# A shared PSUM bank, reordered maxima and query transposes, and other weight loads in a fused attention, expert and gated-product kernel

## The chip, the cores and the metric

One core of one Trainium2 chip runs the whole program. The metric is the device time of one execution, in microseconds. A profiled execution gives a trace: each instruction of TensorE (PE), VectorE (DVE), ScalarE (ACT) and GpSimd (POOL) with its start and duration, and the DMAs that SyncE (SP) issues.

## What is computed

Three parts follow one another; the output of each is the input of the next.

```python
# attention: q, k, v are 2 x 8 x 576 x 64 (batch, heads, positions, 64)
q_d, k_d, v_d = means of q, k, v over 4 neighbouring positions    # 144 positions
out_d = softmax(q_d @ k_d.T / 8) @ v_d, repeated 4 times
out_local = softmax(q @ k.T / 8 where |i - j| < 4, else -1e9) @ v
x = (out_up + out_local) as 1152 tokens x 512
# experts: 8 of them, w1 512 x 1024, w2 1024 x 512
P = exp(x @ w_gate - max);  8 times: P /= row sums; P /= column sums; P *= 1152 / 8
x = sum over e of P[:, e] * (relu(x @ w1[e]) @ w2[e])
# gated product, inner width 1536
out = (x @ w_a) * (x @ w_b) @ w_out
```

## The kernel before

**Precision.** All is float32 outside. For the large products each operand is split into a high part (rounded to fp32r) and a low part (what is left); a product is three matmuls. A piece of weights, `raw`, becomes its two parts in `split` (L134): ScalarE copies the high part (L138), VectorE or GpSimd subtracts it (L139).

**Attention as 24 orders.** An order is one batch, one third of the 576 positions and a pair of heads. The generator `side` (L1268) works them off as a software pipeline of steps s = 0, 1, 2 ...; a step is two halves, and in it several orders are at different stages:

- `a1(s)`: TensorE transposes queries (`qn`, L991) and, when a head pair is new, keys (`kn`, L1005); `a2` (ScalarE) copies them to `qT`, `kT`; `a3` (VectorE) sums four neighbours (`kd`, L1049; `qT`, L1034); `a4` (ScalarE) scales the keys' sums (`kd`, L1060).
- `b1`, `b1c`: TensorE's mask, band scores and coarse scores (all at L61, the one line of `mm`). `b2(s-1)`: VectorE's negated maxima `nm` (L1090) and `nd` (L1093). `b3(s-1)`: ScalarE's exponentials `p` (L1100) and `pd` (L1103).
- `b4(s-2)`: VectorE's sums `rsum` (L1112, L1113) and reciprocals `rr` (L1116); GpSimd multiplies `p` by them (L1117), VectorE `pd`, which gives `pdn` (L1120).
- `c1(s-2)`: TensorE transposes `pdn` (L1130) and `p` (L1135), into two PSUM banks; `c2` and `c3` copy them to `pdT` (L1141) and `plT` (L1149).
- `d1(s-3)`: eight products of `pdT` (into columns 192 to 239 of one bank) and twelve of `plT` (into its columns 0 to 191). `d2a`: ScalarE's `od` (L1170) is a quarter of the columns from 192; `d2`: VectorE's `x` (L1176) adds it to columns 0 to 191. `d3` splits `x` into `xh` (ScalarE, L1186) and `xl` (GpSimd).

So within step s TensorE does `d1(s-3)` and right after it `c1(s-2)`, and ScalarE does `d2a(s-3)` and then `b3(s-1)`. Up to TURN = 11 the scores stand in the first half of a step (`b1(s-1)`), from there on in the second, `b1(s)` in front of `d1` and `b1c(s)` behind it.

**Banks.** The attention's tiles in PSUM have the tag `at`, of 6 banks that go round; 2 more belong to the experts' first products (`g`). A tile of 512 float32 is one bank. An instruction that writes into a bank taken anew waits for the last readers of what lay there.

**What fills TensorE.** The first two half experts ("units" 0 and 1) begin while the attention runs: once tokens are ready, `step` (L1492) works through experts' tiles, calls half a step of `side` from time to time and, by the list `share` (L1490), so many tasks from the queue of weight splits (`run_first`). Loads of weights are asked for one piece per half step in `load_some` (L230), from lists that `halves` and `queue_plain` (L245) make; a piece is half the rows of a 512 x 512 block, two loads of 128 x 512 elements (or 128 x 2 x 256 for the very first unit).

Engines take their instructions strictly in the order of the program; a tile's readers and writers on other engines are kept apart by semaphores.

Of the kernel before, what the change touches and what calls it, by code (L numbers as in the profile page):

```python
# [20 lines left out]
def attn_moe_glu_kernel(  # L21
# [208 lines left out]
    def load_some():  # L230

        if nsteps[0] >= max(6, freed[0] + 2):
            fetch()
        while coming and not coming[0].dmas:
            coming.pop(0)
        if coming and nsteps[0] not in NO_LOAD:
            coming[0].dmas.pop(0)()
# [7 lines left out]
    def queue_plain(u, uses=6, low=None):  # L245

        u.w = {}
        rs = halves(u.load1, (2, 2))
        for i in range(2):
            for j in range(2):  # L250
                def piece(i=i, j=j):
                    b = u.w[i, j] = new_block(uses)
                    split(b, rs[j].tile[:, :, 256 * i:256 * i + 256], 2, low)
                    rs[j].used()
                wq.append(Task(piece, 0.0 if low else 0.68, 1.35 if low else 0.0, ready=rs[j].ready, slot=True))
# [161 lines left out]

    units = []
    for e in range(E):
        for hf in range(2):  # L420
            u = Unit()
            u.e, u.hf = e, hf
            load = loader if units else half_loader
            u.load1 = load(w1[e][:, hf * 512:(hf + 1) * 512].rearrange("(k p) f -> p k f", p=128))
            u.load2 = loader(w2[e][hf * 512:(hf + 1) * 512, :].rearrange("(k p) f -> p k f", p=128))
            units.append(u)
# [557 lines left out]
    pA, pB, pC, pD = {}, {}, {}, {}  # L984

    def a1(i, b, u, hp):
# [3 lines left out]
        for j in range(2):  # L990
            nc.tensor.transpose(  # L991
                pq[:, j * 96:(j + 1) * 96], qn[:, j].rearrange("p h d -> p (h d)"), ident[:96, :96]
            )
        pk = pk2 = None
# [113 lines left out]
    def b4(i, b, u, hp):  # L1108
        p, pd, rs = pB[i]
        rr = at.tile([128, NC + 1], F32, tag="rr", name="rr", bufs=2)  # L1110
        out_ = at.tile([R, SD], F32, tag="pdn", name="pdn", bufs=2)
# [7 lines left out]
        )  # L1119
        nc.vector.tensor_scalar_mul(  # L1120
# [4 lines left out]
    def c1(i, b, u, hp):  # L1125
        p, pd = pB.pop(i)
        pt = psa.tile([128, 512], F32, tag="at", name="at")
        pt2 = psa.tile([128, 512], F32, tag="at", name="at")
# [23 lines left out]
    def d1(i, b, u, hp):  # L1152
        a, d = pC.pop(i)
        hs = slice(2 * hp, 2 * hp + 2)
        ps = psa.tile([128, 512], F32, tag="at", name="at")
        n = NC * 16
# [111 lines left out]
    def side():  # L1268
# [17 lines left out]
        for s in range(n + 5):  # L1286
# [13 lines left out]
            do(a1, s)  # L1300
# [8 lines left out]
            if not last:  # L1309
                do(d3, s - 4)  # L1310
            do(b2, s - 1)
            do(a3, s)
# [14 lines left out]
            do(b3, s - 1)  # L1327
            do(c1, s - 2)
# [44 lines left out]
    with tc.manual_schedule():  # L1373
# [34 lines left out]
        for u, low in zip(units[:2], (nc.gpsimd, None)):  # L1408
            queue_plain(u, low=low)
# [80 lines left out]
        share = [0, 0, 1, 1, 1, 1, 2, 2, 1, 2, 1]  # L1490
# [207 lines left out]
```

## Time and profile before

| | us |
|---|---|
| runs | 1049.03, 1402.92, 1048.74; median 1049.03 |
| the profiled execution, its own time | 1048.58 |
| its span, first to last instruction | 1046.8 |
| TensorE busy | 1037.9 (99%) |
| VectorE, GpSimd, ScalarE busy | 656.1, 528.3, 481.1 |
| granted clock of TensorE, mean | 1.000 |

The profile gives for each engine the time in which it executed instructions. TensorE's matmuls overlap one another (a row of the timeline takes in several, so its end can lie behind the next row's start), so the rows' starts say more than their ends. In a timeline, "[0.91 <-ACT pd L1103]" behind a row is the time for which the engine stood idle before it and what released it. The granted clock is a share of full speed.

### The profile page before, as it was taken

The numbers are of one execution on the slowest core, as the hardware profiler recorded it, in microseconds if no ns is written. First come the engines' busy times: TensorE is split into PE (matmuls) and PEld (weight loads), VectorE is DVE, ScalarE is ACT, GpSimd is POOL, SyncE is SP. The second block draws the span as 40 slices with busy tenths as digits, with TensorE's granted clock in tenths as the row PEclk, the third lists the DMA queues.
The fourth block names the chain that finished last, engine by engine and source line by source line (L and its number), as shares of the span: only waits on it lengthen the run. The fifth ranks groups of instructions, "written<-read, shape, count | busy, mean of one in ns | idle before, by whom it ended". The sixth has DMA issues, their size and how long they took to land.

```text
span 1046.8 us, 18525 instructions
## 1 busy us (share of the span) xinstructions
PE 1037.9 (99%) x6940; PEld 937.7 (90%) x6940; DVE 656.1 (63%) x1328; ACT 481.1 (46%) x1173; POOL 528.3 (50%) x531
## 2 busy tenths in 40 slices
PE   8999999999999999999999999999999999999998
PEld 6888889899899998999899899989999899999997
DVE  7785548666566565656656565656444685767664
ACT  6764424555444444445444454544343744332320
POOL 5633136647464555647364564746444544655521
PEclk9999999999999999999999999999999999999999
DMA  9662001243323323242433323232110101221102
GB/s 194 149 165 62 10 1 41 71 132 94 117 80 115 102 71 106 66 129 83 112 104 88 106 67 113 95 113 82 61 61 21 41 21 61 61 61 41 34 8 90
DMA packets 80728, 84.53 MB, mean 81 GB/s; under 512 B 35328, under 2 KB 54784, under 8 KB 80640
## 3 DMA queue, kind: packets, MB, share of 16 engines
q1 hardware_dynamic: 78864, 82.92, 27.4%
q8 instruction: 54, 0.88, 0.3%
q10 hardware_dynamic: 1776, 0.44, 0.2%
q14 instruction: 34, 0.28, 0.1%
HBM read 71.54 MB, written 11.80 MB: 80 GB/s over the span
## 4 chain that ended last, share of the span: by engine, by line
PE 95%; DVE 2%; POOL 1%; ACT 1%; issue 1%; DMA 0%; DVEq 0%; ACTq 0%; POOLq 0%
PE g L61 90%; PE at L61 3%; PE at L1130 1%; PE at L1135 1%; PE g L855 0%; PE at L991 0%; POOL w L139 0%; PE at L1005 0%; DVE G L696 0%; ACT p L1100 0%; DMA raw<-w 0%; POOL gl L692 0%; DVE kd L1049 0%; DVE b L621 0%; DVE rsum L1112 0%
## 5 line engine op out<-in xcount | busy, mean ns | idle before, releaser
L61 PE MATMUL g<-w,gh 128*128 128x512 f32 x1314 | 408.0, 392 | 0.0
L61 PE MATMUL g<-xh,w 128*128 128x256 f32 (+2 forms) x1472 | 316.0, 300 | 0.0
L692 POOL TENSOR_TENSOR gl<-G,gh 128x256 fp32r<-128x256 f32 (+1 forms) x216 | 177.8, 832 | 250.1 <-ACT gh L690 244.0
L61 PEld LDWEIGHTS g<-w,gh 128*128 128x128 f32 x1314 | 239.6, 188 | 43.6
L61 PE MATMUL g<-w,gl 128*128 128x512 f32 x657 | 257.6, 392 | 0.0
L61 PEld LDWEIGHTS g<-xh,w 128*128 128x128 f32 x1472 | 242.8, 188 | 2.4
L61 PE MATMUL g<-xl,w 128*128 128x256 f32 (+2 forms) x736 | 220.0, 299 | 0.0
L696 DVE TENSOR_TENSOR G<-g,G 128x256 f32<-128x256 f32 (+1 forms) x400 | 168.3, 451 | 68.6 <-PE g L61 34.5
L61 PE MATMUL g<-Th,w 128*128 128x256 f32 (+1 forms) x960 | 207.5, 294 | 0.4 <-DVE G L696 0.3
L139 DVE TENSOR_TENSOR w<-raw,w 128x512 fp32r<-128x512 f32 x129 | 116.2, 910 | 79.4 <-ACT w L138 79.3
L61 PEld LDWEIGHTS g<-Th,w 128*128 128x128 f32 x960 | 159.7, 188 | 3.3 <-issue 1.0
L548 DVE SCALAR_TENSOR_TENSOR acc<-g,P,acc 128x512 f32<-128x512 f32 x126 | 94.2, 748 | 94.9 <-PE g L61 91.6
L61 PEld LDWEIGHTS g<-w,gl 128*128 128x128 f32 x657 | 123.4, 188 | 26.3
L61 PE MATMUL g<-Tl,w 128*128 128x256 f32 (+1 forms) x480 | 140.7, 293 | 0.0
L61 PEld LDWEIGHTS g<-xl,w 128*128 128x128 f32 x736 | 138.2, 188 | 2.6 <-issue 0.2
L690 ACT CAST gh<-G 128x256 fp32r<-128x256 f32 (+1 forms) x216 | 93.6, 433 | 100.7 <-DVE G L706 85.7
L138 ACT CAST w<-raw 128x512 fp32r<-128x512 f32 x181 | 109.6, 620 | 63.4 <-POOL raw L269 48.3
L688 ACT ACTIVATE G<-G 128x256 f32<-128x256 f32 (+1 forms) x168 | 74.2, 442 | 103.1 <-DVE G L696 103.1
L139 POOL TENSOR_TENSOR w<-raw,w 128x512 fp32r<-128x512 f32 x52 | 68.5, 1324 | 57.7 <-ACT w L138 57.7
L61 PEld LDWEIGHTS g<-Tl,w 128*128 128x128 f32 x480 | 90.3, 188 | 2.1
L381 POOL TENSOR_TENSOR dec<-dec 128x384 int32<-128x384 int32 x48 | 49.4, 1029 | 77.7 <-ACT dec L357 52.3
L139 POOL TENSOR_TENSOR w<-s,w 128x512 fp32r<-128x512 f32 x40 | 55.6, 1391 | 21.1 <-ACT w L138 21.0
(179 smaller groups left out, 990.9 us busy)
## 6 DMA issues: line engine op xcount, KB each, us to landing
raw<-in_moe_w_dram SPq DMA_DIRECT2D x128, 256.0 KB
w<-dec SPq DMA_DIRECT2D x48, 192.0 KB
dec<-in_moe_w_a_dram SPq DMA_DIRECT2D x16, 384.0 KB
dec<-in_moe_w_b_dram SPq DMA_DIRECT2D x16, 384.0 KB
dec<-in_moe_w_out_dram SPq DMA_DIRECT2D x16, 384.0 KB
raw<-w SPq DMA_DIRECT2D x48, 128.0 KB
raw<-w SPq DMA_DIRECT2D x12, 256.0 KB
out_dram<-acc SPq DMA_DIRECT2D x9, 256.0 KB
```

What stands on the lines that cost most here:

```text
L61: nc.tensor.matmul(out=o, lhsT=l, rhs=r, start=start, stop=stop, skip_group_check=not check)
L138: nc.scalar.copy(out=hi, in_=raw)
L139: lows.append(lambda: (low or nc.vector).tensor_tensor(out=lo, in0=raw, in1=hi.bitcast(F32), op=ALU.subtract))
L381: nc.gpsimd.tensor_tensor(out=t, in0=t, in1=raw[:, :, 0], op=ALU.add)
L548: nc.vector.scalar_tensor_tensor(out=a, in0=ps, scalar=P[:, tt, u.e:u.e + 1], in1=a, op0=ALU.mult, op1=ALU.add)
L688: nc.scalar.activation(out=src, in_=src, func=AF.Relu)
L690: nc.scalar.copy(out=h, in_=src)
L692: nc.gpsimd.tensor_tensor(out=l, in0=src, in1=h.bitcast(F32), op=ALU.subtract)
L696: nc.vector.tensor_tensor(out=o, in0=bank_, in1=b, op=ALU.add)
L1130: nc.tensor.transpose(pt2[0:72, kh * 128:kh * 128 + R], pd.rearrange("p (t k) -> p k t", k=2)[:, kh], ident[:R, :R],)
L1135: nc.tensor.transpose(pt[0:W, c * 128:(c + 1) * 128], p[:, c], ident)
```

## The change

- **One bank fewer.** `d1(i)` leaves its bank in `shared[i + 1]`, and `c1(i + 1)` writes the pdn transposes into columns 256 to 511 of it instead of into a bank of its own.
- **Maxima in front of pdn.** The multiplication that makes `pdn` is a stage of its own, `b4d`; in steps below TURN it comes behind `b2`, from there on in front of it as before.
- **Next queries in front of the probabilities.** `a1` keeps the two query transposes, `a1k` has the keys; in steps 1 to 9 `a1(s + 1)` stands in front of `c1(s - 2)`.
- **Loads.** Unit 1's first weights come by halves of the columns (`column_loader`, rows of 1 KB), so that each of the four blocks of the split needs one load piece; after half step 2 * TURN + 1 two loads are asked for at a time; `share` is another list.

```diff
--- before.py
+++ after.py
@@ -234,7 +234,9 @@
         while coming and not coming[0].dmas:
             coming.pop(0)
         if coming and nsteps[0] not in NO_LOAD:
-            coming[0].dmas.pop(0)()
+            for _ in range(2 if nsteps[0] > 2 * TURN + 1 else 1):
+                if coming[0].dmas:
+                    coming[0].dmas.pop(0)()
 
     def halves(load, left):
 
@@ -242,7 +244,7 @@
         lq.extend(rs)
         return rs
 
-    def queue_plain(u, uses=6, low=None):
+    def queue_plain(u, uses=6, low=None, columns=False):
 
         u.w = {}
         rs = halves(u.load1, (2, 2))
@@ -250,9 +252,16 @@
             for j in range(2):
                 def piece(i=i, j=j):
                     b = u.w[i, j] = new_block(uses)
-                    split(b, rs[j].tile[:, :, 256 * i:256 * i + 256], 2, low)
-                    rs[j].used()
-                wq.append(Task(piece, 0.0 if low else 0.68, 1.35 if low else 0.0, ready=rs[j].ready, slot=True))
+                    if columns:
+                        r = rs[i]
+                        raw = r.tile[:, j].rearrange("p (k f) -> p k f", k=2)
+                    else:
+                        r = rs[j]
+                        raw = r.tile[:, :, 256 * i:256 * i + 256]
+                    split(b, raw, 2, low)
+                    r.used()
+                r = rs[i if columns else j]
+                wq.append(Task(piece, 0.0 if low else 0.68, 1.35 if low else 0.0, ready=r.ready, slot=True))
 
     def queue_combined(u, low=None):
 
@@ -415,12 +424,23 @@
 
         return load
 
+    def column_loader(src):
+        def load(t, i):
+            d = t.rearrange("p a (b c) -> p (a b) c", b=2)
+            return [
+                lambda k=k: nc.sync.dma_start(
+                    out=d[:, 2 * k:2 * k + 2], in_=src[:, 2 * k:2 * k + 2, 256 * i:256 * i + 256]
+                ) for k in range(2)
+            ]
+
+        return load
+
     units = []
     for e in range(E):
         for hf in range(2):
             u = Unit()
             u.e, u.hf = e, hf
-            load = loader if units else half_loader
+            load = (half_loader, column_loader)[len(units)] if len(units) < 2 else loader
             u.load1 = load(w1[e][:, hf * 512:(hf + 1) * 512].rearrange("(k p) f -> p k f", p=128))
             u.load2 = loader(w2[e][hf * 512:(hf + 1) * 512, :].rearrange("(k p) f -> p k f", p=128))
             units.append(u)
@@ -981,7 +1001,7 @@
         )
         v_d[b, hp] = vd
 
-    pA, pB, pC, pD = {}, {}, {}, {}
+    pA, pB, pC, pD, shared = {}, {}, {}, {}, {}
 
     def a1(i, b, u, hp):
 
@@ -991,6 +1011,10 @@
             nc.tensor.transpose(
                 pq[:, j * 96:(j + 1) * 96], qn[:, j].rearrange("p h d -> p (h d)"), ident[:96, :96]
             )
+        pA[i] = pq
+
+    def a1k(i, b, u, hp):
+        pq = pA[i]
         pk = pk2 = None
         if not i:
             warm(1)
@@ -1108,7 +1132,6 @@
     def b4(i, b, u, hp):
         p, pd, rs = pB[i]
         rr = at.tile([128, NC + 1], F32, tag="rr", name="rr", bufs=2)
-        out_ = at.tile([R, SD], F32, tag="pdn", name="pdn", bufs=2)
         nc.vector.tensor_reduce(out=rs[:, 0:NC], in_=p_[i % 2], axis=AX.X, op=ALU.add)
         nc.vector.tensor_reduce(
             out=rs[0:R, NC:NC + 1], in_=pd_in[i % 2].rearrange("p g t -> p (g t)"), axis=AX.X, op=ALU.add
@@ -1117,6 +1140,11 @@
         nc.gpsimd.tensor_tensor(
             out=p, in0=p, in1=rr[:, 0:NC].unsqueeze(2).to_broadcast([128, NC, W]), op=ALU.mult
         )
+        pB[i] = p, pd, rr
+
+    def b4d(i, b, u, hp):
+        p, pd, rr = pB[i]
+        out_ = at.tile([R, SD], F32, tag="pdn", name="pdn", bufs=2)
         nc.vector.tensor_scalar_mul(
             out=out_.rearrange("p (g t) -> p g t", g=3), in0=pd, scalar1=rr[0:R, NC:NC + 1]
         )
@@ -1124,8 +1152,11 @@
 
     def c1(i, b, u, hp):
         p, pd = pB.pop(i)
+        pt2 = shared.pop(i, None)
+        if pt2 is None:
+            pt2 = psa.tile([128, 512], F32, tag="at", name="at")
+        pt2 = pt2[:, 256:512]
         pt = psa.tile([128, 512], F32, tag="at", name="at")
-        pt2 = psa.tile([128, 512], F32, tag="at", name="at")
         for kh in range(2):
             nc.tensor.transpose(
                 pt2[0:72, kh * 128:kh * 128 + R],
@@ -1153,6 +1184,8 @@
         a, d = pC.pop(i)
         hs = slice(2 * hp, 2 * hp + 2)
         ps = psa.tile([128, 512], F32, tag="at", name="at")
+        if i + 1 < len(order):
+            shared[i + 1] = ps
         n = NC * 16
         pd_ = ps[:, UT:UT + n]
         for kh in range(2):
@@ -1297,7 +1330,9 @@
             if s in LOAD_V:
                 load_v(LOAD_V[s])
             last = s >= 4 and (s - 3) % (2 * HP) == 0
-            do(a1, s)
+            if s in (0, 1) or s >= TURN:
+                do(a1, s)
+            do(a1k, s)
             if s <= TURN:
                 do(b1, s - 1)
                 do(b1c, s - 1)
@@ -1308,7 +1343,11 @@
             do(b4, s - 2)
             if not last:
                 do(d3, s - 4)
+            if s >= TURN:
+                do(b4d, s - 2)
             do(b2, s - 1)
+            if s < TURN:
+                do(b4d, s - 2)
             do(a3, s)
             if s >= TURN:
                 scale.append(lambda: do(a4, s))
@@ -1325,6 +1364,8 @@
                 do(b1c, s)
             do(d2a, s - 3)
             do(b3, s - 1)
+            if 1 <= s < TURN - 1:
+                do(a1, s + 1)
             do(c1, s - 2)
             do(d2, s - 3)
             do(c2, s - 2)
@@ -1406,7 +1447,7 @@
 
 
         for u, low in zip(units[:2], (nc.gpsimd, None)):
-            queue_plain(u, low=low)
+            queue_plain(u, low=low, columns=u is units[1])
         for u in units[:2]:
             queue_out(u)
         queue_combined(units[2], nc.gpsimd)
@@ -1487,7 +1528,7 @@
         tmp_stack = ExitStack()
         turn = 0.0
         nside = 0
-        share = [0, 0, 1, 1, 1, 1, 2, 2, 1, 2, 1]
+        share = [0, 0, 1, 1, 3, 1, 1, 1, 2, 1, 1]
 
         def step():
             nonlocal turn
```

The order on TensorE in the fourth step (s = 3), around the transposes of `pdn`, first before and then after the change (lines shift by 20 to 33; L1011 and L1161 are what L991 and L1130 were):

```order
L61 MATMUL at<-plT,vw 64x64 x2
L1130 MATMUL at<-ident,pdn 72x112 [waits DVE_49,PE_49]
L1130 MATMUL at<-ident,pdn 72x112
L1135 MATMUL at<-ident,p_115 70x128 [waits Pool_49]
L1135 MATMUL at<-ident,p_115 70x128 x2
L991 MATMUL at<-ident,qn 128x96 [waits DMAHW1_49,DMAHW0_49,PE_49]
L991 MATMUL at<-ident,qn 128x96
```

```order
L61 MATMUL at<-plT,vw 64x64 x2
L1011 MATMUL at<-ident,qn 128x96 [waits DMAHW1_49,DMAHW0_49,PE_49]
L1011 MATMUL at<-ident,qn 128x96
L1161 MATMUL at<-ident,pdn 72x112 [waits DVE_49,Activation_49]
L1161 MATMUL at<-ident,pdn 72x112
L1166 MATMUL at<-ident,p_115 70x128 [waits Pool_49]
L1166 MATMUL at<-ident,p_115 70x128 x2
```

The next step's query transposes moved ahead of the first pdn transpose, and this one waits for a semaphore of ScalarE where it waited for one of its own engine.

On VectorE, in the fifth step (s = 4), the reductions to `nm` and `nd` and the multiplication to `pdn`, before and after:

```order
L1116 RECIPROCAL rr<-rsum_120 128x4 [waits DVE_49]
L1120 TENSOR_SCALAR pdn<-pd_116,rr 112x144 [waits DVE_49]
L1090 TENSOR_REDUCE nm<-at 128x3 [waits PE_49]
L1093 TENSOR_REDUCE nd<-at 112x1
L1049 TENSOR_REDUCE kd_446<-kT_429 128x144 [waits Activation_49]
L1034 TENSOR_REDUCE qT_112<-qT_112 128x48 [waits Activation_49]
L1176 TENSOR_TENSOR x<-at,od 128x192 [waits Activation_49]
```

```order
L1139 RECIPROCAL rr<-rsum_120 128x4 [waits DVE_49]
L1114 TENSOR_REDUCE nm<-at 128x3 [waits PE_49]
L1117 TENSOR_REDUCE nd<-at 112x1
L1148 TENSOR_SCALAR pdn<-pd_116,rr 112x144 [waits DVE_49]
L1073 TENSOR_REDUCE kd_445<-kT_428 128x144 [waits Activation_49]
L1058 TENSOR_REDUCE qT_112<-qT_112 128x48 [waits Activation_49]
L1209 TENSOR_TENSOR x<-at,od 128x192 [waits PE_49,Activation_49]
```

`pdn` moved behind the two maxima, still in front of the keys' reduction; `x` waits for TensorE in addition.

On ScalarE, the splits of weights (`w<-raw`) in front of the `od` of orders 10 and 11, before and after:

```order
L500 ACTIVATE gh_97<-g_1206 128x384 [waits PE_49]
L138 CAST w_1221<-raw 128x512
L500 ACTIVATE gh_97<-g_1224 128x384 [waits PE_49]
L138 CAST w_1239<-raw 128x512
L1170 ACTIVATE od<-at 128x48 [waits PE_49,Activation_49]
...
L1060 ACTIVATE kd_1322<-kd_1322 128x144 [waits DVE_49]
L138 CAST w_1341<-raw 128x512 [waits DMAHW6_49]
L138 CAST w_1345<-raw 128x512 [waits DMAHW4_49]
L1170 ACTIVATE od<-at 128x48 [waits PE_49,Activation_49]
```

```order
L520 ACTIVATE gh_97<-g_1199 128x384 [waits PE_49]
L138 CAST w_1214<-raw 128x512 [waits DMAHW7_49]
L138 CAST w_1217<-raw 128x512 [waits DMAHW0_49]
L138 CAST w_1220<-raw 128x512 [waits DMAHW6_49]
L520 ACTIVATE gh_97<-g_1223 128x384 [waits PE_49]
L138 CAST w_1238<-raw 128x512 [waits DMAHW7_49]
L1203 ACTIVATE od<-at 128x48 [waits PE_49,Activation_49]
...
L1084 ACTIVATE kd_1321<-kd_1321 128x144 [waits DVE_49]
L138 CAST w_1340<-raw 128x512 [waits DMAHW0_49]
L1203 ACTIVATE od<-at 128x48 [waits PE_49,Activation_49]
```

Two splits moved from the steps of orders 11 and 12 forward to that of order 10, and there three stand in one row, each with a wait for its own load.

## Rows read from the trace of the kernel before

**Rows 1.** The page, part 1: TensorE's busy time, share of the span, instructions.

```profile
PE 1037.9 (99%) x6940; PEld 937.7 (90%) x6940; DVE 656.1 (63%) x1328; ACT 481.1 (46%) x1173; POOL 528.3 (50%) x531
```

**Rows 2.** Table by stretches of time: busy us of each engine, granted clock, DMA share, GB/s.

```profile
core 0: us, PE busy (x) PEld busy (x) DVE busy (x) ACT busy (x) POOL busy (x), PEclk, DMA share, GB/s
...
11.20:20.50 9.30, 8.29 (x144) 6.66 (x142) 7.87 (x29) 7.12 (x29) 5.81 (x9) 1.00 1.07 211
20.50:37.93 17.43, 17.29 (x275) 14.53 (x273) 14.22 (x48) 15.53 (x59) 15.07 (x23) 1.00 0.71 158
...
61.60:63.40 1.80, 0.89 (x11) 0.70 (x9) 1.38 (x5) 1.80 (x8) 0.69 (x1) 1.00 0.60 189
63.40:127.00 63.60, 63.60 (x662) 55.15 (x661) 42.15 (x119) 32.35 (x111) 19.62 (x28) 1.00 0.26 68
127.00:1042.40 915.40, 914.63 (x5508) 832.24 (x5507) 565.90 (x1048) 403.15 (x907) 474.46 (x444) 1.00 0.25 75
```

**Rows 3.** Timeline of TensorE (start, us, engine, line, tiles): orders 20 and 21.

```profile
115.33 0.28 PE L61 MATMUL at<-pdT,vd 72*64 72x48 f32 x4
115.44 0.53 PE L61 MATMUL at<-plT,vw 70*64 70x64 f32 x12
...
116.15 0.42 PE L1130 MATMUL at<-ident,pdn 112*72 112x112 f32 x2
...
121.72 0.42 PE L1130 MATMUL at<-ident,pdn 112*72 112x112 f32 x2
```

**Rows 4.** Timeline of ScalarE, the same steps.

```profile
116.08 0.21 ACT L1170 ACTIVATE od<-at 128x48 f32<-128x48 f32 x1 [0.74 <-PE at L61]
...
121.90 0.21 ACT L1170 ACTIVATE od<-at 128x48 f32<-128x48 f32 x1 [0.31 <-PE at L61]
```

**Rows 5.** Timeline of ScalarE, orders 11 and 12.

```profile
61.47 0.62 ACT L138 CAST w<-raw 128x512 fp32r<-128x512 f32 x1 [0.49 <-DMA raw<-in_moe_w_dram]
61.99 0.20 ACT L1170 ACTIVATE od<-at 128x48 f32<-128x48 f32 x1
...
62.70 0.40 ACT L1103 ACTIVATE pd<-at,nd 112x144 f32<-112x144 f32 x1
...
67.40 0.21 ACT L1170 ACTIVATE od<-at 128x48 f32<-128x48 f32 x1
```

**Rows 6.** Timeline of TensorE, orders 11 and 12.

```profile
61.07 0.42 PE L1130 MATMUL at<-ident,pdn 112*72 112x112 f32 x2
...
63.15 0.47 PE L1005 MATMUL at<-ident,kn 96*128 96x96 f32 x3 [0.91 <-ACT pd L1103]
...
67.07 0.42 PE L1130 MATMUL at<-ident,pdn 112*72 112x112 f32 x2
```

**Rows 7.** Timeline of ScalarE in the first steps.

```profile
17.67 0.19 ACT L1170 ACTIVATE od<-at 128x48 f32<-128x48 f32 x1
...
20.38 0.74 ACT L1100 ACTIVATE p<-at,nm 128x70 f32<-128x70 f32 x3 [0.33 <-DVE nd L1093]
...
24.12 0.19 ACT L1170 ACTIVATE od<-at 128x48 f32<-128x48 f32 x1
...
36.79 0.21 ACT L1170 ACTIVATE od<-at 128x48 f32<-128x48 f32 x1
```

**Rows 8.** Timeline of TensorE in the first steps.

```profile
17.41 0.52 PE L1135 MATMUL at<-ident,p 128*70 128x128 f32 x3 [0.37 <-POOL p L1117]
17.77 0.33 PE L991 MATMUL at<-ident,qn 96*128 96x96 f32 x2
18.02 0.28 PE L61 MATMUL at<-mask,identb 64*64 64x210 bf16 x2
...
23.03 0.42 PE L1130 MATMUL at<-ident,pdn 112*72 112x112 f32 x2
23.28 0.49 PE L1135 MATMUL at<-ident,p 128*70 128x128 f32 x3
...
35.74 0.42 PE L1130 MATMUL at<-ident,pdn 112*72 112x112 f32 x2
```

**Rows 9.** Timeline of VectorE in the first steps.

```profile
28.37 0.36 DVE L1120 TENSOR_SCALAR pdn<-pd,rr 112x144 f32<-112x144 f32 x1
28.65 0.37 DVE L1090 TENSOR_REDUCE nm<-at 128x3 f32<-128x210 f32 x1
...
35.15 0.38 DVE L1090 TENSOR_REDUCE nm<-at 128x3 f32<-128x210 f32 x1 [0.57 <-PE at L61]
```

## The prediction

> **What bounds the kernel now.** I read the page's busy shares first: TensorE works in 99% of the span [rows 1]. The table by stretches then shows where the rest lies: from 63.40 us to 127.00 us TensorE is busy for all of 63.60 us, at a granted clock of 1.00 (its upper level, 2.4 GHz); from 20.50 to 37.93 us it lacks 17.43 - 17.29 = 0.14 us; in the 1.80 us from 61.60 to 63.40 us it is busy for 0.89 us only [rows 2]. So after some 20 us the path runs through TensorE nearly without a gap: whatever makes it wait there is added to the time, and only its own idle time can be won. The change moves no matmul out of the program (as many as before, of the same shapes), and behind the attention, in the last 915 us, every engine's order is the same. The sum is therefore one of waits, in the first 130 us.
>
> I call the 24 attention pieces orders 0 to 23. Order k has its products in step k+3, and there its `od` copy on ScalarE, and the transposes of the probabilities of order k+1 follow on TensorE.
>
> **The shared bank: what waits.** After the change the pdn transposes write columns 256 to 511 of the bank whose columns 0 to 239 hold the products just made. The reordered program shows what that brings: the first pdn transpose waits for ScalarE besides VectorE, where before it waited for VectorE and its own engine; the semaphore's count is that of `od` in the same step. So at 23 places (each order but the last hands its bank on) TensorE has to stand until `od` has read. That the wait goes by the bank is seen in the trace too: `od` reads columns that the eight pdT products write, and of these the last four are issued from 115.33 us for 0.28 us, so they end at 115.61 us; but `od` starts at 116.08 us, 0.11 us after the last plT product has ended (115.44 + 0.53 = 115.97 us) [rows 3, 4].
>
> The Trainium skill ("PSUM — Partial Sum Buffer", section "PSUM bank collisions raise a hardware error") has the rule that PSUM is to be guarded by bank and quadrant and not by address, since two engines on different columns of one bank still collide. The start of `od` above agrees with it; no run here shows the collision itself. It speaks against this change: by the rule the transposes can't run beside `od`, and by addresses alone they could, which is the first rival below.
>
> **The price in the late steps (orders 8 to 22).** In an ordinary one TensorE begins the pdn transposes at 116.15 us, while `od` runs from 116.08 for 0.21 us, to 116.29 us [rows 3, 4]. How long it takes from a release to TensorE's start I read at another place: the `pd` exponential ends at 62.70 + 0.40 = 63.10 us, and TensorE, which waited for it, starts at 63.15 us, so 0.05 us [rows 5, 6]. The transposes then start at 116.34 instead of 116.15 us: +0.19 us. Eleven orders (8 to 10, 13 to 20) have this pattern, within 0.02 us: 11 x 0.19 = 2.1 us. In orders 21 and 22 no scores stand between the products and the transposes; these began at 121.72 us and `od` ends at 121.90 + 0.21 = 122.11 us, so 122.16 - 121.72 = 0.44 us, twice: 0.9 us.
>
> In orders 11 and 12 `od` was late, behind splits of weights on ScalarE: it ended at 61.99 + 0.20 = 62.19 us where the transposes began at 61.07 us, and at 67.40 + 0.21 = 67.61 us where they began at 67.07 us [rows 5, 6]. Were that so still, the new wait would cost 62.24 - 61.07 = 1.17 and 67.66 - 67.07 = 0.59 us. But the new list `share` puts two splits forward to the step at 53 us, so that one split stands in front of `od` where there were two, here and in order 12. One split needs 0.52 us of ScalarE (61.47 to 61.99, the next start), and without the second one, and its wait of 0.49 us for its load, `od` of order 11 comes when the products are done, as in the other steps. I take 0.19 for each, 0.4 us together, and keep 1.17 + 0.59 = 1.8 us as the upper end; the lower end is 0. Late steps: 2.1 + 0.9 + 0.4 = 3.4 us.
>
> **What one bank fewer gives.** At 63.15 us the key transposes waited 0.91 us, until ScalarE had read a bank of scores [rows 6]. With one bank fewer taken per step that wait should go, since those transposes no longer need the bank of that step: -0.91 us. Its ends are -0.91 and 0. No other stall after 20.5 us is as long: the stretch up to 37.93 us has 0.14 us in all.
>
> **The first eleven steps.** Three edits meet here: the shared bank, the next step's query transposes in front of the pdn transposes (cover for the new wait: 0.25 us, from 17.77 to 18.02 us [rows 8]), and the maxima in front of pdn on VectorE. In most steps the wait is small (order 2: products, `od`, and transposes lie as in the late steps), the moved query transposes fill 0.25 us of it, and I set them at 0. In three steps, those in which new keys come, `od` stands on ScalarE behind the scaling of the keys' sums, and this behind VectorE's reduction; there it is late and TensorE, in order, waits:
> - Order 1: `od` ends at 17.67 + 0.19 = 17.86 us, so the pdn transposes start at 17.91 us. The p transposes follow 0.25 us later (23.03 to 23.28 us), and the mask products 0.36 us after these (17.41 to 17.77 us, the queries now being ahead): 18.52 instead of 18.02 us, +0.50. This is less than the delay of the pdn transposes, since the p transposes waited for GpSimd until 17.41 us anyway [rows 7, 8].
> - Order 3: `od` ends at 24.12 + 0.19 = 24.31 us; the pdn transposes start at 24.36 instead of 23.03 us, 1.33 later, of which the 0.25 us of queries are cover: +1.08.
> - Order 7: `od` ends at 36.79 + 0.21 = 37.00 us. Here VectorE had pdn done before the 0.57 us in which it waited for TensorE's scores; now pdn stands behind the maxima, and the keys' reduction starts later by its pitch, 0.28 us (28.37 to 28.65 us) [rows 9]. So 37.00 + 0.28 + 0.05 = 37.33 instead of 35.74 us; in this step no queries are moved: +1.59.
>
> Together 0.50 + 1.08 + 1.59 = 3.2 us. The bounds are wide: nothing (if the delay only takes the place of waits that TensorE has anyway) to 3.9 us (if the 0.25 us of cover is worth nothing in any of the three). Below zero: the maxima come 0.28 us sooner, and ScalarE's exponentials waited for them 0.33 us at 20.38 us [rows 7]; three steps have such a wait (0.27 to 0.33 us), so at best -0.9 us. But in these steps TensorE's next work hangs on `od`, which the earlier maxima don't bring forward, and I take nothing for it.
>
> **The loads.** Unit 1's first weights come as four pieces of 256 columns instead of by rows, two pieces per half step are asked for after half step 23, and on SyncE's queue pieces of the second weights now stand in front of some loads of queries and keys. TensorE waits for no weight there (63.60 of 63.60 us busy [rows 2]), and the queries are asked for two steps ahead. I set them at 0. If a load comes late, ScalarE waits for it as it did for 0.49 us at 61.47 us [rows 5]; beneath 0 nothing can come of them, as nothing waits for them on the path.
>
> **The sum.** 3.4 - 0.9 + 3.2 = +5.7, in exact terms 2.09 + 0.88 + 0.38 - 0.91 + 3.17 = 5.6 us. The profiled execution took 1048.58 us (span 1046.8 us, 1.8 us around it); 1048.58 + 5.6 = 1054.2 us. The median of the three runs before, 1049.03 us, lies 0.45 us above the profiled execution, which I leave out. A measurement of this kernel can tell about 2%, 21 us, from no change: the forecast is a small loss within that bound.
>
> **Rivals.**
> - The transposes don't wait for `od` in practice (other side: not slower). By addresses they could run beside it. Then the late steps cost nothing, the 0.91 us at 63 us goes, and the earlier maxima give up to 0.9 us: 1048.58 - 1.8 = 1046.8 us. It decides if TensorE starts pdn before `od` ends. For it: the columns differ. Against it: the wait stands in the order, and the 0.11 us of `od`. Chance 0.14.
> - The early waits are absorbed: up to 20 us VectorE and ScalarE set the pace, and TensorE's wait for `od` takes the place of waits that would have come later in the step (as for GpSimd at 17.41 us). Then 2.5 us from the late steps and at most 0.5 of the early ones: 1048.58 + 2.0 to 3.0, 1051 us. Against it: from 20.5 to 37.93 us TensorE has 0.14 us of slack, so orders 3 and 7 have little to absorb them. Chance 0.2.
> - Loads come late: the three splits that now stand in one row at 53 us wait for their weights on ScalarE, whose queue holds `od` and the exponentials, or the queries, moved forward, wait for theirs. Then orders 11 and 12 cost 1.8 instead of 0.4 us and one wait of 0.49 us comes on top: 1054.2 + 1.4 + 0.5 = 1056.1 us. For it: the wait at 61.47 us. Chance 0.13.
> - The clock falls in a stretch with stalls. A step of about 3 us at the lower level (1.2 GHz) would take twice that: 1057.2 us. Against it: the stretch with 0.91 us of idle in 1.80 us was granted 1.00 [rows 2]. Chance 0.03.
>
> The forecast itself has 0.5. Its own range is 1051.5 to 1056.5 us; with the rivals, 1046.7 to 1057.3 us, which takes in the first and the last of them. All of it lies within 2% of the time before (1028 to 1070 us), so: faster by over 2% 0.005, within 2% 0.985, slower 0.01.
>
> **What would show it.** Right: `od` followed by the pdn transposes 0.05 us later in every step; TensorE's waits for ScalarE's `od` of about 0.2 us in orders 8 to 20, and of 1 us and more in orders 3 and 7; no wait of the key transposes at about 63 us; the end of the attention some 5.6 us later, and the rest as long as before. Wrong: pdn transposes that start while `od` runs; TensorE idle in the first 40 us no more than before; or a difference that arises after 130 us, where I have none.

## The result and the profile after

| | before | after |
|---|---|---|
| median of 6 runs each, us | 1048.88 | 1056.38 |
| ratio, 95% interval | | 1.0067 [1.0052, 1.0081] |
| profiled execution: its time, span | 1048.58, 1046.8 | 1056.37, 1054.6 |

The kernel became slower by 0.67%, about 7 us, which the interval tells from no change; 1054.2 us were forecast. One run on either side, far above the others, counts in no interval. The other runs after the change lie at two places, 1054.6 us with a mean granted clock of 1.000 and 1056.4 us with 0.998; the profiled execution is one of the latter, and the difference between the two places is the one term that the forecast did not have.

TensorE works as many instructions as before and is still the engine that sets the time. The page's row of busy shares, which answers to [rows 1], has 3.7 us more of busy time on it, though the work is the same (part of it is a slower clock, as the table below shows):

```profile
PE 1041.6 (99%) x6940; PEld 938.9 (89%) x6940; DVE 655.8 (62%) x1328; ACT 483.8 (46%) x1173; POOL 528.2 (50%) x531
```

The table by stretches (start to end, TensorE's busy us, and behind the engines the granted clock). The first row is cut at the same times as in [rows 2]. The second ends where TensorE goes on behind order 7, which was at 35.74 us before. The last three lie about where [rows 2] has its last three:

```profile
core 0: us, PE busy (x) PEld busy (x) DVE busy (x) ACT busy (x) POOL busy (x), PEclk, DMA share, GB/s
11.20:20.50 9.30, 7.96 (x140) 6.21 (x139) 7.01 (x27) 6.93 (x27) 5.26 (x8) 1.00 0.96 205
20.50:39.48 18.98, 16.11 (x250) 12.79 (x250) 13.34 (x47) 15.27 (x56) 15.28 (x24) 1.00 0.59 146
...
40.50:43.50 3.00, 3.00 (x24) 2.29 (x24) 1.75 (x8) 1.27 (x4) 1.59 (x4) 0.50 0.63 175
...
67.50:69.50 2.00, 2.00 (x19) 2.00 (x17) 1.81 (x8) 1.98 (x7) 0.99 (x2) 1.00 0.59 133
69.50:133.70 64.20, 62.31 (x647) 53.11 (x646) 39.81 (x112) 31.86 (x105) 19.14 (x28) 1.00 0.22 59
133.70:1050.00 916.30, 915.72 (x5514) 832.99 (x5515) 567.07 (x1050) 403.49 (x907) 474.36 (x444) 1.00 0.25 75
```

From 20.50 to 39.48 us TensorE now lacks 2.87 us, where it lacked 0.14 us; from 40.50 to 43.50 us it is busy throughout but was granted 0.50 of full speed, its lower level of 1.2 GHz; the stretch around the key transposes is full (2.00 of 2.00 us, before 0.89 of 1.80); from 69.50 to 133.70 us 1.89 us are missing, before none; and the rest is as it was. The list of what TensorE waited for (total us, times, longest) puts a name to it that did not exist before:

```profile
PE at L1161 <- ACT od L1203: 4.3, 5, 1.5
```

`L1161` are the pdn transposes and `od L1203` the copy that reads the bank they write into. (The list names 5 of the 23 places; at the other late ones a start some 0.2 us later shows it.) Where the time arose is seen best from the starts of the same matmuls in both traces:

| place in the program | before, us | after, us | later by |
|---|---|---|---|
| products of order 0 | 12.61 | 12.71 | 0.10 |
| mask products behind order 1 | 18.02 | 18.84 | 0.82 |
| products of order 3 | 22.18 | 22.91 | 0.73 |
| mask products behind order 3 | 24.39 | 26.25 | 1.86 |
| products of order 7 | 35.01 | 37.16 | 2.15 |
| pdn transposes behind order 7 | 35.74 | 39.48 | 3.74 |
| products of order 8 | 43.93 | 49.21 | 5.28 |
| products of order 11 | 60.14 | 65.99 | 5.85 |
| pdn transposes behind order 11 | 61.07 | 67.11 | 6.04 |
| products of order 12 | 66.14 | 71.05 | 4.91 |
| products of order 21 | 120.99 | 127.82 | 6.83 |
| products of order 23 | 129.29 | 137.03 | 7.74 |
| the last matmul | 1042.42 | 1050.15 | 7.73 |

The loss comes in three jumps behind orders 1, 3 and 7, in one of 1.54 us in which nothing waits (the clock), and in small, nearly even steps from order 8 on. From the products of order 11 to those of order 12, 0.94 us come back. After the attention nothing changes.

The timeline of TensorE behind orders 1, 3 and 7, to be laid beside [rows 8]; the last row is a group of twelve score products that took 0.53 us elsewhere:

```profile
18.16 0.42 PE L1161 MATMUL at<-ident,pdn 112*72 112x112 f32 x2 [1.03 <-ACT od L1203]
...
18.84 0.28 PE L61 MATMUL at<-mask,identb 64*64 64x210 bf16 x2
...
25.05 0.42 PE L1161 MATMUL at<-ident,pdn 112*72 112x112 f32 x2 [1.03 <-ACT od L1203]
...
39.48 0.42 PE L1161 MATMUL at<-ident,pdn 112*72 112x112 f32 x2 [1.51 <-ACT od L1203]
...
41.46 0.90 PE L61 MATMUL at<-kT,qT 128*64 128x70 f32 x12
```

and ScalarE's `od` of these orders, beside [rows 7]; 38.87 us is the scaling that stands in front of the third:

```profile
17.92 0.19 ACT L1203 ACTIVATE od<-at 128x48 f32<-128x48 f32 x1
...
24.81 0.19 ACT L1203 ACTIVATE od<-at 128x48 f32<-128x48 f32 x1
...
38.87 0.32 ACT L1084 ACTIVATE kd<-kd 128x144 f32<-128x144 f32 x1 [0.55 <-DVE kd L1073]
39.22 0.21 ACT L1203 ACTIVATE od<-at 128x48 f32<-128x48 f32 x1
```

Each time the transposes start 0.05 us after `od` ends (17.92 + 0.19 = 18.11, 18.16; 24.81 + 0.19 = 25.00, 25.05; 39.22 + 0.21 = 39.43, 39.48 us). On VectorE `pdn` stands behind the maximum that had to wait for the scores, beside [rows 9]: it is issued at 37.82 us, and the keys' reduction, for which the scaling waits, starts 0.27 us after it.

```profile
37.31 0.38 DVE L1114 TENSOR_REDUCE nm<-at 128x3 f32<-128x210 f32 x1 [1.05 <-PE at L61]
...
37.82 0.35 DVE L1148 TENSOR_SCALAR pdn<-pd,rr 112x144 f32<-112x144 f32 x1
38.09 0.74 DVE L1073 TENSOR_REDUCE kd<-kT 128x144 f32<-128x576 f32 x1
```

The late steps, orders 20 and 21, on TensorE and then on ScalarE, beside [rows 3] and [rows 4]:

```profile
122.90 0.41 PE L1161 MATMUL at<-ident,pdn 112*72 112x112 f32 x2
...
128.99 0.42 PE L1161 MATMUL at<-ident,pdn 112*72 112x112 f32 x2 [0.37 <-ACT od L1203]
```

```profile
122.64 0.21 ACT L1203 ACTIVATE od<-at 128x48 f32<-128x48 f32 x1 [0.74 <-PE at L61]
...
128.73 0.21 ACT L1203 ACTIVATE od<-at 128x48 f32<-128x48 f32 x1 [0.31 <-PE at L61]
```

122.64 + 0.21 + 0.05 = 122.90 us: exactly the step that was worked out. Order 11, beside [rows 5] and [rows 6]: one split in front of `od` instead of two, no wait for a load, and the six key transposes come as one group, without a gap.

```profile
66.22 0.61 ACT L138 CAST w<-raw 128x512 fp32r<-128x512 f32 x1
66.85 0.21 ACT L1203 ACTIVATE od<-at 128x48 f32<-128x48 f32 x1
...
67.56 0.40 ACT L1127 ACTIVATE pd<-at,nd 112x144 f32<-112x144 f32 x1
```

```profile
67.86 0.66 PE L1029 MATMUL at<-ident,kn 96*128 96x96 f32 x6
```

### The profile page after: what moved, and what is told of

Read it like the earlier page. It is cut to its first block, busy times and chain, and to the rows that moved or that the text cites. A ratio compares the mean times of both kernels' runs of the same rounds, so it can differ in the third digit from the quotient of the medians.

```text
span 1054.6 us, 18532 instructions
## 1 busy us (share of the span) xinstructions
PE 1041.6 (99%) x6940; PEld 938.9 (89%) x6940; DVE 655.8 (62%) x1328; ACT 483.8 (46%) x1173; POOL 528.2 (50%) x531
## 4 chain that ended last, share of the span: by engine, by line
PE 95%; DVE 2%; ACT 1%; POOL 1%; issue 1%; DMA 0%; ACTq 0%; POOLq 0%; DVEq 0%
PE g L61 90%; PE at L61 3%; PE at L1161 1%; PE at L1166 1%; ACT od L1203 0%; PE at L1029 0%; PE g L875 0%; POOL w L139 0%; PE at L1011 0%; ACT w L138 0%; DMA raw<-w 0%; DVE kd L1073 0%; POOL gl L712 0%; DVE G L716 0%; DVE b L641 0%
```

## The experiments

Theory at the start: the loss is TensorE's wait for `od` on the shared bank, plus the clock that falls after the longest of these waits. Rivals: the reordering costs by itself; the loads do; the clock falls for a reason of its own. Each comparison has its own runs of the kernel before beside it (medians 1048.48 to 1048.65 us).

**Own bank, all else of the change kept.**

```diff
-        if i + 1 < len(order):
-            shared[i + 1] = ps
```

> The changed kernel, but the pdn transposes write into a bank of their own as before the change; everything else of the change stays. Theory (the loss is the wait for od on the shared bank, and what the clock does after the longest of these waits): no wait of TensorE for od, the key transposes wait some 0.9 us at about 63 us again; 1048.0 to 1049.5 us, within 0.7 us of the kernel before. Rival (the reordered maxima and query transposes or the loads cost time by themselves): 1051 us or more.

1049.4 us, ratio 1.0007 [0.9998, 1.0017] to the kernel before: not told apart from it (0.9 us above it by the medians, for 0.7 expected at most), and 5 or 7 us under the two places of the changed kernel. TensorE doesn't wait for `od` any more. One part of the expectation was wrong: the key transposes at 63 us don't wait either, though every tile has its own bank again. Two further things are in its trace. Behind order 7 the pdn transposes wait for `pdn`, which is late behind the maxima:

```profile
38.30 0.39 PE L1161 MATMUL at<-ident,pdn 112*72 112x112 f32 x2 [0.35 <-DVE pdn L1148]
```

And in this execution TensorE's first matmuls ran slow until 10.45 us, which put it 1.7 us behind the changed kernel at the second group of score products (10.60 against 8.87 us). Twelve score products took 0.91 us instead of 0.53:

```profile
6.88 0.91 PE L61 MATMUL at<-kT,qT 64*64 64x70 f32 x12
```

That is the pace which such a group had in the stretch granted 0.50 (0.90 us). The trace's records of the granted clock begin at 10.35 us in this execution, with full speed, and at 4.72 us in the kernel before; ahead of them a row shows 1.00 for want of any record. Whether the edit has a part in that slow start, no run shows. The ten runs form two groups, six between 1048.62 and 1049.55 us and four between 1050.04 and 1050.36 us, and this execution is the slowest of them; that the other three of its group began as late is likely, but not shown.

**The shared bank alone**, in the kernel before (the line that makes `shared` an empty dictionary is left out here):

```diff
+        pt2 = shared.pop(i, None)
+        if pt2 is None:
+            pt2 = psa.tile([128, 512], F32, tag="at", name="at")
+        pt2 = pt2[:, 256:512]
         pt = psa.tile([128, 512], F32, tag="at", name="at")
-        pt2 = psa.tile([128, 512], F32, tag="at", name="at")
...
         ps = psa.tile([128, 512], F32, tag="at", name="at")
+        if i + 1 < len(order):
+            shared[i + 1] = ps
```

> The kernel before with the shared bank alone; pdn, the query transposes, loads and splits stay as they were. Theory: the same waits for od as in the changed kernel: late steps 0.19 us each and 0.44 us in the last two, minus 0.9 to 1.1 us at 63 us; orders 1, 3 and 7 without the cover of the query transposes 0.75, 1.3 and 1.3 us, and orders 11 and 12 up to 1.2 and 0.6 us, since the splits of weights stand in front of od there; 1053.5 to 1056.5 us at a granted clock of 1.00, 1.8 us more in runs in which the clock falls. Rival (the loss comes of the combination): under 1052 us.

1055.89 us (1055.54 to 1056.06), ratio 1.0069 [1.0056, 1.0083], and the clock at 0.999 to 1.000 in all runs: the shared bank by itself loses 7.4 us, as much as the whole change, and without a fall of the clock. Without the moved query transposes and with two splits in front of `od` TensorE waits longer for it, 6.6 us in all:

```profile
PE at L1133 <- ACT od L1175: 6.6, 11, 1.2
```

In orders 11 and 12 the pdn transposes come 0.59 and 0.63 us later still (from 4.44 to 5.03 us and from 3.92 to 4.55 us behind the kernel before), so the new splits do help the changed kernel there. For order 12 the 0.59 us that were worked out nearly hold; for order 11 it is half of the 1.17 us, since the two splits follow each other without a wait for a load in this trace.

**The shared bank from order 8 on only**, own banks before:

```diff
-        if i + 1 < len(order):
+        if 8 <= i < len(order) - 1:
             shared[i + 1] = ps
```

> The changed kernel, with the shared bank from the products of order 8 on only; before that own banks. Theory: the three long waits of the first eleven steps and the fall of the clock behind the third are gone, the late 0.19 us stay: 2.5 us more than e1 less what the key transposes get back, 1050.5 to 1051.5 us, clock 1.000. Rival (the late waits are hidden or the early loss has another source): 1048 us, or 1053 us and more.

1052.79 us, above the expected range. Against the run with own banks throughout (1049.4 us) it is 3.4 us: the late waits alone, 3.4 us as in the prediction. The two profiled executions, which both began late (clock records from 10.35 and 9.88 us), differ by 3.3 us. What was wrong in the expectation is the 0.9 us taken off: they had already gone with own banks.

**Work for TensorE while it waits.** Twelve products of ones in front of the pdn transposes of order 8; they write a bank that the p transposes then overwrite.

```diff
+        for _ in range(12 if i == 8 else 0):
+            mm(pt[:, :256], wz[:, 0:128], wz, True, True)
         for kh in range(2):
```

> The changed kernel with twelve idle products of 128 x 256 bfloat16 ones in front of the pdn transposes of order 8, where TensorE stands 1.5 us waiting for od of order 7; they write a bank that the p transposes overwrite. Theory (the clock fell because TensorE stood still there): the granted clock is 1.000 in every run and the time is that of the changed kernel's runs without the fall, 1054.4 to 1054.8 us. Rival (the clock falls for another reason, for instance the load that comes after): 1056.4 us at 0.998 in most runs, as in the changed kernel.

1054.79 us; all five runs lie between 1054.71 and 1055.26 us, none at 1056.4. The transposes start at 39.46 us, as late as before (39.48 us), so the wait for `od` is the same; only TensorE isn't idle in it. The score products behind it take 0.53 us, and the clock stays at 1.00:

```profile
37.88 1.48 PE L61 MATMUL at<-wz 128*128 128x256 bf16 x12
39.46 0.42 PE L1163 MATMUL at<-ident,pdn 112*72 112x112 f32 x2
...
40.94 0.53 PE L61 MATMUL at<-kT,qT 128*64 128x70 f32 x12
```

```profile
40.50:43.50 3.00, 3.00 (x33) 2.65 (x32) 2.18 (x8) 1.31 (x5) 1.60 (x4) 1.00 0.58 147
```

From those transposes to the products of order 8 nothing is lost (3.72 us and 3.73 us later than before), where the first trace of the changed kernel lost 1.54 us. So the 1.8 us between the two places of the changed kernel are not the wait itself, but the clock. That it falls because TensorE stands still is what this run speaks for. It isn't proof: the changed kernel's clock fell in 5 of 11 runs (below), and at that rate five runs without a fall come by chance in about 5 of 100 cases.

**The p transposes in front of the pdn transposes**, all else as in the changed kernel:

```diff
+        for c in range(NC):
+            nc.tensor.transpose(pt[0:W, c * 128:(c + 1) * 128], p[:, c], ident)
         for kh in range(2):
             nc.tensor.transpose(
                 pt2[0:72, kh * 128:kh * 128 + R],
...
-        for c in range(NC):
-            nc.tensor.transpose(pt[0:W, c * 128:(c + 1) * 128], p[:, c], ident)
```

> The changed kernel, with the p transposes in front of the pdn transposes in each step; the bank stays shared. Theory (TensorE loses what od needs because pdn stands right behind the products): the three p transposes, 0.33 us, cover the 0.19 us of the late steps wholly and 0.33 us of each longer wait, so some 2.4 us in the orders 8 to 20, 0.66 us in orders 21 and 22 and 0.9 us in orders 1, 3 and 7 come back: 1050.5 to 1051.5 us with the clock at 1.000. Rival (the later pdn transposes delay pdT and with it the next products): 1053 us or more.

1050.18 us (1050.03 to 1050.46), ratio 1.0015 [1.0006, 1.0024]: 4.4 us under the faster place of the changed kernel (1054.6), a little more than expected. In a late step TensorE has the p transposes to do while `od` runs, and the pdn transposes follow without a wait:

```profile
80.97 0.52 PE L1161 MATMUL at<-ident,p 128*70 128x128 f32 x3
81.33 0.36 PE L1163 MATMUL at<-ident,pdn 112*72 112x112 f32 x2
```

```profile
80.90 0.21 ACT L1203 ACTIVATE od<-at 128x48 f32<-128x48 f32 x1 [2.09 <-PE at L61]
```

`od` ends at 81.11 us, 0.22 us ahead of the transposes' start.

**The loads and the list of splits alone**, in the kernel before: the diff's first three parts on `load_some`, `queue_plain` and `column_loader`, and the new `share`.

> The kernel before with the loads and the list of splits alone; own banks, maxima and query transposes as before. Theory (the key transposes' wait of 0.91 us at 63 us goes because the split that stood in front of od of order 11, and its wait for a load, stand elsewhere; it has nothing to do with the number of banks): no such wait, 0.9 us under the kernel before, 1047.3 to 1047.9 us. Rival (that wait went with the other parts): as the kernel before, 1048.3 to 1048.7 us.

1048.0 us, ratio 0.9998 [0.9989, 1.0006]: the median is 0.5 us below the kernel before, and the interval doesn't tell them apart. Ten of the eleven runs lie between 1047.48 and 1048.75 us. The eleventh took 1051.36 us at a mean granted clock of 0.997, lower than in any run of the changed kernel; that execution has no trace, so the cause stays open. The mechanism is there: one split, then `od`, and the key transposes in one piece.

```profile
61.15 0.61 ACT L138 CAST w<-raw 128x512 fp32r<-128x512 f32 x1
61.78 0.21 ACT L1201 ACTIVATE od<-at 128x48 f32<-128x48 f32 x1
...
62.49 0.40 ACT L1127 ACTIVATE pd<-at,nd 112x144 f32<-112x144 f32 x1
```

```profile
62.60 0.81 PE L1029 MATMUL at<-ident,kn 96*128 96x96 f32 x6
```

In the profiled execution 0.98 us come back there, and 0.5 us are lost at 26 us in a wait for values that is not in the trace of the kernel before. Whether the new loads cause it stays open. Such waits come without them too: the run with the list alone, whose loads are the old ones, waits for keys at 21 us.

```profile
21.27 0.69 PE L1005 MATMUL at<-ident,kn 96*128 96x96 f32 x6 [0.39 <-DMA kn<-in_k_dram]
```

**pdn in front of the maxima again**, all else as in the changed kernel:

```diff
-            if s >= TURN:
-                do(b4d, s - 2)
+            do(b4d, s - 2)
             do(b2, s - 1)
-            if s < TURN:
-                do(b4d, s - 2)
```

> The changed kernel with pdn in front of the maxima in all steps as before; bank shared, query transposes moved, loads changed. Theory: TensorE's wait for od in order 7 is shorter by the 0.28 us of pdn, 1.2 us; the rest as in the changed kernel: 1054.3 us at clock 1.000, and if the clock falls after a wait of 1.2 us too, 1056.1 us. Rival (the earlier maxima save time in the first steps): 1055.0 us and more at 1.000.

1054.36 us (1054.12 to 1054.50), as expected to 0.1 us; four runs of four without a fall of the clock. The wait behind order 7 is 0.27 us shorter, and that is what the place of `pdn` costs the changed kernel:

```profile
39.17 0.42 PE L1161 MATMUL at<-ident,pdn 112*72 112x112 f32 x2 [1.24 <-ACT od L1203]
```

**The two moves alone**, own banks, loads and splits as before: the parts of the diff on `a1k`, `b4d` and their places in `side`.

> The kernel before with the two moves alone (maxima in front of pdn, next queries in front of the probabilities); own banks, loads and splits as before. Theory: without the loads the key transposes wait at 63 us again, 0.9 us over e1: 1049.5 to 1050.3 us, with 0.6 to 0.9 us lost in the first eleven steps, where pdn comes later. Rival (the moves are free and e1's loss is of the loads): 1048.5 us.

1049.72 us, ratio 1.001 [1.0001, 1.0019]: the moves cost about 1.2 us by themselves. In the trace TensorE is 0.64 us late at the products of order 7, 1.07 us at those of order 8 and 1.37 us at those of order 12; the last 0.3 us arise at the key transposes, which wait again, for 1.19 us instead of 0.91, behind the two splits and their load:

```profile
62.80 0.62 ACT L138 CAST w<-raw 128x512 fp32r<-128x512 f32 x1 [0.76 <-DMA raw<-in_moe_w_dram]
```

```profile
64.48 0.47 PE L1029 MATMUL at<-ident,kn 96*128 96x96 f32 x3 [1.19 <-ACT pd L1127]
```

**The changed kernel once more.** No edit.

> The changed kernel itself, once more, for how often its clock falls. Theory (the fall after TensorE's 1.5 us wait for od of order 7 is worth 1.8 us and comes in some executions only): two groups of runs, 1054.5 to 1054.8 us with the clock near 1.000 and 1056.3 to 1056.5 us at about 0.998, and nothing between. Rival (a steady loss): one group.

Two of six runs at 1056.57 and 1056.59 us with the clock at 0.998, four between 1054.65 and 1055.48 us. With the first series that is 5 of 11 runs in which the clock fell (3 of 5 there). The lower group is wider than expected. Its slowest run, 1055.48 us, is the profiled execution, and its trace has no fall. At the products of order 3 it is already 0.45 us behind the first trace (23.36 against 22.91 us), for a reason that isn't shown. The wait for `od` is as long:

```profile
39.92 0.42 PE L1161 MATMUL at<-ident,pdn 112*72 112x112 f32 x2 [1.51 <-ACT od L1203]
```

```profile
40.00:42.00 2.00, 2.00 (x28) 1.76 (x28) 1.49 (x6) 1.92 (x8) 1.35 (x3) 1.00 0.72 157
42.00:44.00 2.00, 2.00 (x15) 1.90 (x12) 1.22 (x4) 0.33 (x2) 0.93 (x3) 1.00 0.71 200
```

So the same wait of 1.51 us brings the lower level in one execution and not in another.

**The list of splits alone**, in the kernel before:

```diff
-        share = [0, 0, 1, 1, 1, 1, 2, 2, 1, 2, 1]
+        share = [0, 0, 1, 1, 3, 1, 1, 1, 2, 1, 1]
```

> The kernel before with the new list of splits alone; loads as before. Theory: one split less in front of od of orders 11 and 12 is all that was to be had, so the key transposes' 0.91 us at 63 us go without the other parts: 1047.4 to 1047.8 us, the fastest of all. Rival (without the column pieces the three splits in a row at 53 us find no weights loaded and hold up od of order 10, or the loads of values are late as in the run with the loads alone): 1048.3 us and more.

1052.08 us, ratio 1.0031 [1.0019, 1.0043]: the rival was right. Without the column pieces the third split in the row finds no weights and waits 2.92 us for them, with `od` of order 10 and the exponentials behind it; the key transposes then wait 2.48 us, and the clock falls, in all five runs (mean 0.998):

```profile
57.48 0.62 ACT L138 CAST w<-raw 128x512 fp32r<-128x512 f32 x1 [2.92 <-DMA raw<-in_moe_w_dram]
...
58.90 0.21 ACT L1170 ACTIVATE od<-at 128x48 f32<-128x48 f32 x1
```

```profile
60.06 0.74 PE L1005 MATMUL at<-ident,kn 96*128 96x96 f32 x3 [2.48 <-ACT pd L1103]
```

```profile
57.00:59.00 2.00, 0.59 (x7) 0.40 (x5) 0.87 (x2) 1.52 (x5) 0.00 (x0) 1.00 0.98 263
...
61.00:63.00 2.00, 2.00 (x8) 2.00 (x7) 1.96 (x6) 1.14 (x4) 1.27 (x3) 0.50 1.10 192
```

## Why the prediction was right, and where not

**The wait for `od`: right, in place and size.** The transposes follow `od` by 0.05 us in each of the places shown. Late steps, by the starts of the products: 0.16 to 0.27 us each in orders 8 to 20 without order 11, 0.2 us in the mean (0.19 worked out), and 0.47 and 0.44 us in orders 21 and 22 (0.44 worked out). In order 11 the wait costs nothing in the end: from its products to those of order 12 the kernel with own banks gets back as much as the changed kernel (0.95 and 0.94 us). The run with the shared bank in the late steps alone gives 3.4 us for the 3.4 of the sum. First steps: order 3 cost 1.86 - 0.73 = 1.13 us (forecast 1.08), order 7 3.74 - 2.15 = 1.59 (1.59). Order 1 was mis-sized: 0.70 instead of 0.50 us (0.82 less the 0.12 us by which its products were late already); `od` starts there at 17.92 instead of 17.67 us. I had seen the delay by `pdn` behind the maxima in order 7 alone; in order 1 too the maximum now waits for scores (0.53 us), and with `pdn` behind it the keys' reduction starts at 16.91 instead of 16.66 us. About 0.12 us of this is the lateness from before. (With `pdn` in front again it also starts at 16.91 us, in an execution that was 0.29 us late by then; so the cause fits, but isn't shown by itself.)

```profile
16.13 0.38 DVE L1114 TENSOR_REDUCE nm<-at 128x3 f32<-128x210 f32 x1 [0.53 <-PE at L61]
...
16.91 0.74 DVE L1073 TENSOR_REDUCE kd<-kT 128x144 f32<-128x576 f32 x1
```

The rivals of no wait at all and of absorbed waits both fall. The upper bound of 3.9 us for these three steps had a slip: it counts the cover of the queries three times, and order 7 has none, so it should be 3.7 us.

**"What one bank fewer gives": the size, but not the only cause.** The 0.91 us came back: 5.85 - 4.91 = 0.94 us from the products of order 11 to those of order 12. Orders 8 to 23 as a whole, with this, cost 7.74 - 5.28 = 2.46 us, for 2.5 in the forecast. But the run with own banks and the one with loads alone don't have that wait either, so the split that stood in front of `od`, and its load, are enough to explain it: the exponential `pd`, which frees the bank, comes sooner. The shared bank alone also removes it: there the list of TensorE's waits has none at the key transposes, and TensorE is 3.92 us behind at the products of order 12, after 4.44 us at those of order 11. So either part suffices; it is counted once. In the changed kernel the sharing therefore gives nothing that the loads and the list don't, and its price there is some 5 us without the clock (1054.6 less 1049.4).

**"I set them at 0": not quite.** The other steps up to order 7 add 0.12 us before order 1 and 2.15 - 1.86 = 0.29 us behind order 3, and give back 0.82 - 0.73 = 0.09 us between them: 0.3 us. The moves alone cost 1.2 us by the medians; that the changed kernel adds only 0.3 us beside its waits for `od` fits with most of it lying under them. One part is separated: with `pdn` in front again the changed kernel gets back 0.27 us behind order 7, and the 0.29 us behind order 3 stay, so these are not of `pdn`. The mechanism in one place is shown: `pdn` behind the maxima, which wait for scores, makes the pdn transposes wait (0.35 us behind order 7 with own banks).

**The loads: right** as to the sum; ScalarE's three splits in a row do not wait: they stand in one group of 1.65 us from 58.85 us, without a gap.

```profile
58.85 1.65 ACT L138 CAST w<-raw 128x512 fp32r<-128x512 f32 x3
```

Of the third rival, late loads, one part did happen in the changed kernel, and cost next to nothing: TensorE waits 0.43 us for queries that were moved forward, and the products of order 1 come only 0.12 us later than before. The splits did not wait; the run with the list alone shows that this part of the mechanism is real.

```profile
10.40 0.61 PE L1011 MATMUL at<-ident,qn 96*128 96x96 f32 x2 [0.43 <-DMA qn<-in_q_dram]
```

**The clock: a rival that came in addition.** I gave it 0.03 as a case of its own, with the argument that 0.91 us of idle in 1.80 had been granted full speed. That argument failed: the wait that the forecast itself put behind order 7, 1.5 us, is longer than any wait after 20 us in the trace that I read, so the trace could not speak for it. The price was 1.54 us in the profiled execution and 1.8 us between the two places of the runs, less than the 3 us taken. Without it the changed kernel takes 1054.55 to 1055.48 us, the forecast's 1054.2 us plus 0.35 us or more; with it 1056.4. That the median of 1056.38 us still lies under the 1056.5 us of the forecast's own range, by 0.1 us, is luck: the upper end of that range was not worked out with the clock. It also lies near the third rival's 1056.1 us, whose splits did not wait.

Point by point: sum without the clock 5.6 us, measured in the trace 7.73 - 1.54 = 6.19 us; of the 0.6 us more, 0.2 us are from order 1, 0.05 from order 3 and 0.3 from the other early steps.

None of the versions tried is shown to be faster than the kernel before. The one with the loads and the list alone has the lowest median, 6.6 us under the faster place of the changed kernel.

## What to carry to other kernels

Before two producers are put into one bank, list the readers of its first half and what stands in front of them on their engine: the second producer waits for the last of them, and its delay is that whole queue, not the copy. If the bank must be shared, put independent work of TensorE between the two (here the p transposes, 0.36 us from start to start, which took back 4.4 us). A wait that grows beyond any that the trace has shown may also cost in the matmuls behind it, so it should be filled or cut.

## What the runs showed of the chip

After TensorE stood still for 1.51 us it was granted 0.50 of full speed for some 3 us in one profile, and 1.00 in another with the same wait; by time and mean clock it fell in 5 of 11 executions. With a longest wait of 2.48 us it fell in 5 of 5; with one of 1.24 us (pdn in front again; the shared bank alone) in none of 8; with the 1.51 us filled by idle products in none of 5. So the fall goes with the length of the idle time in these kernels, but doesn't follow from it alone, and one run with the loads alone had a low clock for a reason that no trace shows. The records of the granted clock begin between 3.71 and 10.35 us in the twelve traces, with full speed. Where they begin at 10.35 us, twelve score products at 6.88 us took 0.91 us; where they begin at 4.72 us, the same products at 6.12 us took 0.53 us.
